# Attention times v in plain fp32 on two column tiles of TensorE, one a head

## The chip, the core and the metric

The kernel runs on one core of a Trainium2 chip. The metric is the time of one execution in microseconds (us), the median over executions. The core has five engines that run side by side: TensorE (PE; its weight loads are shown apart as PEld), VectorE (DVE), ScalarE (ACT), GpSimd (POOL) and SyncE (SP), which issues all of this kernel's DMAs. TensorE's clock is granted at one of two levels, 1.2 or 2.4 GHz; the profile gives the granted clock as a share of 2.4 GHz.

## The reference

```python
q_rot, k_rot = (rotate(q), rotate(k))                     # 4 batches, 8 heads, 576 positions, 64 wide
scores = scale * np.matmul(q_rot, k_rot.transpose(0, 1, 3, 2))
scores = scores - np.max(scores, axis=-1, keepdims=True)
attn = np.exp(scores)
attn = attn / (np.sum(attn, axis=-1, keepdims=True) + 1e-09)
x = np.matmul(attn, v)                                    # heads side by side: 2304 x 512
h = x @ w_in                                              # 512 x 2048
P = a[0] + a[1] * h + a[2] * h**2 + a[3] * h**3
Q = 1.0 + np.abs(b[0]) * np.abs(h) + np.abs(b[1]) * h**2
out = (P / (Q + 1e-06)) @ w_out                           # 2048 x 512
```

Attention with rotated q and k comes first, then a feed-forward part with a rational function in the place of an activation. All is fp32.

## The kernel before

**Attention** goes over 16 pairs of heads; 16 pairs take 16 turns. For a pair p these steps are made, each a named step of the program:

- `ld`, `ro0` to `ro2`: load q and k, rotate them (GpSimd). `hi` (ScalarE) writes the rounded half of q and k into the buffer `q2`, `lo` (GpSimd) what is left over, as fp32r. The DMAs `kh`, `kl` move k's halves from `q2` to `ks`, and `qh`, `ql` then copy q's halves over the place in `q2` where k's halves stood, so `qh` waits until `kh` has landed and `ql` until `kl` has. `q2` has two buffers: `hi` of pair p waits for the last scores of pair p-2. There are two buffers for loaded x, given back by `lo`.
- `s0` to `s8` (line 453): the scores, nine blocks of 128 rows for the two heads together; 42 matmuls a pair. `m0` to `m8` take the row maxima (VectorE, line 461), `x0` to `x8` the exponentials and their sums (ScalarE, line 468). The score banks in PSUM are two.
- `tA`, `tB`, `tJ`, `tL` (line 511): 45 transposes of 128 columns in eleven groups, most of four, one PSUM bank a group, three banks. `hA`, `hB`, ... (ScalarE, line 528) copy a bank's rounded half to `eh`, `lA`, `lB`, ... (VectorE, line 530) write what is left over to `el`; both must be done before the bank is free.
- `vh` and `vl` (ScalarE and GpSimd, lines 431 and 434) split v in the same way into `vv`, the halves side by side: 128 columns.
- `av0` to `av3` (line 541): for each head and half of the positions ten matmuls of 288 columns, five with `eh` and five with `el`, against `vv`. So the sum with v's high half comes out in 64 rows of the bank and that with its low half in the other 64. `ac` (ScalarE) copies the lower rows out, `aa` (VectorE) adds the two. There is one such bank.
- `n0` to `n4`: the reciprocal sums, turned by a transpose (`n1`, line 480), sent to DRAM and back spread over 64 rows (`n3`, `n4`). `f0` (GpSimd) multiplies by them, `f1` stores the result for the feed-forward part.

**Feed-forward** runs in 73 units. A unit has twelve matmuls of 512 columns into a bank `h` (line 816), a chain of some twelve steps on ScalarE, VectorE and GpSimd, and twelve matmuls into four banks `acc` (lines 864 to 866). Its weights come in a packed form and take some six steps each on ScalarE, VectorE and GpSimd before they can be used. The first units `h0` to `h3` stand between the last steps of attention, because the banks `acc` need the PSUM that attention gives back after its last `av`.

**Order.** Nothing on the chip chooses: each engine takes its instructions in the order written. That order comes from a table of due times (`SLOTS`, in ninths of a turn, with tables of their own for pairs 0, 1, 14 and 15, and `DUE` for the feed-forward part) and from a planner that goes through the steps with a time for each; the due times give the order in which ready steps are taken. The times in the planner are the author's and are not used here as evidence.

Of the kernel before, what the change touches and what calls it, by code (L numbers as in the profile page):

```python
# [1140 lines left out]
```

## Time and profile before

| | |
|---|---|
| time, median of 3 executions | 721.39 us (719.87 to 724.22) |
| span of the profiled execution, first to last instruction | 718.0 us |
| TensorE busy | 680.2 us (95%) |
| VectorE busy | 578.5 us (81%) |
| ScalarE busy | 584.9 us (81%) |
| GpSimd busy | 447.8 us (62%) |
| mean granted clock of TensorE | 0.985 |

The profile's span ends at the last instruction and has no time of its own for what lies around it; the median of the shown executions is 3.4 us above it. Busy time is an average over stages. Matmuls overlap in the pipeline and their ends are modelled, so the pace of TensorE is read from the distance between starts, not from the duration of one.

### The profile page before, as it was taken

The page shows a single profiled execution, that of the slowest core. Times are in us where ns is not written, and L with a number is a line of the kernel's source. Part 1 is how long each engine was busy: PE and PEld are TensorE (multiplying, and loading weights), DVE is VectorE, ACT ScalarE, POOL GpSimd, SP SyncE. Part 2 cuts the span into 40 slices and gives each one's busy share as a digit, 9 for nine tenths or more (in the row PEclk, how much of TensorE's full clock was granted, in tenths as well). Part 3 has the DMA queues.
Part 4 walks back from the last instruction along what each step waited for, and adds up shares of the span by engine and source line. Part 5 has one row for each costly group of instructions (what it writes and reads, how often), then busy time and mean ns, then how long its engine had stood idle before and what let it go on. Part 6 is the DMA issues. An engine that isn't in the chain of part 4 may idle for free.

```text
span 718.0 us, 11373 instructions
## 1 busy us (share of the span) xinstructions
PE 680.2 (95%) x3864; PEld 586.6 (82%) x3864; DVE 578.5 (81%) x941; ACT 584.9 (81%) x1110; POOL 447.8 (62%) x295
## 2 busy tenths in 40 slices
PE   6698999999999998969999999999999999999997
PEld 2587998999999997858787888888888888888896
DVE  5798888989889989997998998986766667666685
ACT  1598899999999999987998997988777777776774
POOL 0567778788788847486676766767544554444422
PEclk9699999999999999989999999999999999999999
DMA  9758787887887665352434234323100010000100
GB/s 251 213 123 212 176 210 189 191 194 193 216 188 212 162 186 178 106 174 104 150 115 147 89 132 146 119 97 124 51 0 1 7 45 16 0 1 0 48 13 30
DMA packets 34649, 86.34 MB, mean 120 GB/s; under 512 B 5008, under 2 KB 8224, under 8 KB 32672
## 3 DMA queue, kind: packets, MB, share of 16 engines
q1 hardware_dynamic: 34592, 85.62, 42.8%
q8 instruction: 31, 0.51, 0.3%
q14 instruction: 26, 0.21, 0.1%
HBM read 55.25 MB, written 12.66 MB: 95 GB/s over the span
## 4 chain that ended last, share of the span: by engine, by line
PE 72%; DMA 14%; ACT 5%; DVE 5%; issue 1%; POOL 1%; SPq 1%; DVEq 0%; POOLq 0%; ACTq 0%
PE h L816 26%; PE acc L866 9%; PE acc L865 9%; PE acc L864 9%; PE s L453 7%; DMA ks<-q 7%; PE av L541 6%; DMA q<-q 4%; PE t_B L511 3%; ACT e L468 2%; PE t_A L511 2%; DMA const<-in_b_dram 1%; ACT eh L528 1%; PE t_J L511 1%; DMA tab<-in_tab_dram 1%
## 5 line engine op out<-in xcount | busy, mean ns | idle before, releaser
L453 PE MATMUL s<-ks,q 128*128 128x288 f32 (+2 forms) x672 | 121.4, 311 | 22.4 <-DVE ks L402 8.5
L849 POOL TENSOR_TENSOR gl<-u,gh 128x512 fp32r<-128x512 f32 (+1 forms) x73 | 93.8, 1286 | 75.9 <-ACT gh L848 59.8
L840 POOL TENSOR_TENSOR v<-v,t 128x512 f32<-128x512 f32 x68 | 88.6, 1303 | 83.9 <-ACT v L838 82.8
L461 DVE TENSOR_REDUCE nm<-s 128x1 f32<-128x576 f32 x144 | 107.9, 752 | 24.5 <-PE s L453 22.3
L453 PEld LDWEIGHTS s<-ks,q 128*128 128x128 f32 x672 | 97.0, 194 | 30.1 <-ACT e L468 11.2
L468 ACT ACTIVATE e<-s,nm 128x576 f32<-128x576 f32 x144 | 107.0, 743 | 12.8 <-DVE nm L461 8.3
L541 PE MATMUL av<-eh,vv 128*128 128x288 f32 x320 | 91.3, 308 | 6.5 <-DVE xo L558 6.5
L866 PE MATMUL acc<-woh,gl 128*128 128x512 f32 x234 | 92.4, 395 | 0.2 <-POOL gl L849 0.2
L865 PE MATMUL acc<-wol,gh 128*128 128x512 f32 x234 | 92.4, 395 | 0.0
L864 PE MATMUL acc<-woh,gh 128*128 128x512 f32 x234 | 92.3, 394 | 0.0
L541 PE MATMUL av<-el,vv 128*128 128x288 f32 x320 | 87.7, 297 | 0.0
L837 ACT ACTIVATE t<-h 128x512 f32<-128x512 f32 (+1 forms) x73 | 43.1, 591 | 47.4 <-PE h L816 47.1
L845 DVE SCALAR_TENSOR_TENSOR v<-v,p 128x512 f32<-128x512 f32 (+1 forms) x73 | 49.5, 678 | 39.2 <-ACT p L844 37.8
L841 DVE TENSOR_TENSOR u<-u,h 128x512 f32<-128x512 f32 (+1 forms) x73 | 49.5, 678 | 37.4 <-ACT u L839 37.1
L816 PE MATMUL h<-xh,wih 128*128 128x512 f32 (+1 forms) x204 | 75.1, 368 | 0.1
L816 PE MATMUL h<-xh,wil 128*128 128x512 f32 (+1 forms) x204 | 74.9, 367 | 0.0
L816 PE MATMUL h<-xl,wih 128*128 128x512 f32 (+1 forms) x204 | 74.7, 366 | 0.0
L379 POOL TENSOR_TENSOR x<-x,tab 128x1152 f32<-128x1152 f32 x28 | 74.4, 2663 | 0.0
L541 PEld LDWEIGHTS av<-eh,vv 128*128 128x128 f32 x320 | 60.7, 190 | 7.7 <-ACT xh L789 3.9
L848 ACT ACTIVATE gh<-u 128x512 fp32r<-128x512 f32 (+1 forms) x73 | 45.5, 623 | 20.1 <-PE acc L865 15.2
L541 PEld LDWEIGHTS av<-el,vv 128*128 128x128 f32 x320 | 61.0, 191 | 0.0
L838 ACT ACTIVATE v<-t,const 128x512 f32<-128x512 f32 (+1 forms) x73 | 59.1, 809 | 2.0
(114 smaller groups left out, 1721.6 us busy)
## 6 DMA issues: line engine op xcount, KB each, us to landing
x<-in_qk_dram SPq DMA_DIRECT2D x15, 1152.0 KB
ks<-q SPq DMA_DIRECT2D x30, 288.0 KB, 5.7
q<-q SPq DMA_DIRECT2D x30, 288.0 KB, 4.6
rawi<-in_w_in_dram SPq DMA_DIRECT2D x16, 512.0 KB
rawo<-in_w_out_dram SPq DMA_DIRECT2D x16, 512.0 KB, 3.5
vf<-in_v_dram SPq DMA_DIRECT2D x16, 320.0 KB, 7.5
rb<-rd SPq DMA_DIRECT2D x32, 144.0 KB, 3.8
xd<-xo SPq DMA_DIRECT2D x16, 288.0 KB, 2.1
```

The source lines that it names most:

```text
L379: eng.tensor_tensor(x[:, :, i], x[:, :, i], t, ALU.mult)
L453: nc.tensor.matmul(ps[:, half, x:x + k.shape[-1]], q, k, start=(i == 0), stop=(i == len(ops) - 1))
L461: self.nc.vector.tensor_reduce(nm, st["s", c][:, :, :HALF], AX.XY, ALU.max, negate=True)
L468: self.nc.scalar.activation(e.rearrange("p (a b) -> p a b", a=2), st["s", c][:, :, :HALF], AF.Exp, bias=st["nm", c], scale=1.0, accum_out= ...
L541: nc.tensor.matmul(po[:, :HALF], v, e, start=(i == 0), stop=(i == len(ops) - 1))
L816: self.nc.tensor.matmul(ph[:, i * n:(i + 1) * n], w[:, k * P:(k + 1) * P], x[:, :n], start=(j == 0), stop=(j == len(terms) - 1))
L838: "v": lambda: act(new("v"), d["t"], AF.Identity, bias=self.b[0], scale=self.b[1]),
L840: "w": lambda: (nc.gpsimd.tensor_tensor if u < POOL_W else tt)(d["v"], d["v"], d["t"], ALU.mult),
L849: "gl": lambda: (nc.gpsimd.tensor_tensor(new("gl", F32R), d["u"], fp(d["gh"]), ALU.subtract), self.g.update({u: (d["gh"], d["gl"])})),
L864: nc.tensor.matmul(acc, gh[:, c], hi, start=(first and i == 0), stop=False)
L865: nc.tensor.matmul(acc, gh[:, c], lo, start=False, stop=False)
L866: nc.tensor.matmul(acc, gl[:, c], hi, start=False, stop=(last and i == len(fs) - 1))
```

## The change

`av` has two steps a pair in place of four, one for each half of the positions. In each, ten plain fp32 matmuls write 64 rows each, head 0 to rows 0 to 63 of the bank (column tile 0 of TensorE), head 1 to rows 64 to 127 (column tile 1), in turn. Their operands are the exponentials and v as they are. So `vh`, `vl`, all eleven `l` steps, the four `aa` and two of the four `ac` are gone. A transposed bank is copied out once: five of the eleven groups by ScalarE (`ON_ACT`), six by VectorE. `ac0` copies a finished bank on ScalarE, `ac1` on VectorE. The reordering of head 1's positions, which `aa` did on the way, is now done by the DMAs: `n4` has three DMAs and not two, `f1` three and not one. v's buffers are two (from one), given back after `av`. All due times are set anew.

```diff
-    "s1": -68.81, "s3": -68.34, "ld": -67.83, "s2": -67.47, "s0": -65.53, "s4": -65.09, "s5": -64.79,
...
+    "s1": -66.68, "s2": -66.17, "s3": -64.59, "s0": -64.09, "s4": -63.78, "s5": -63.24, "tA3": -62.77,
...
+ON_ACT = ("A0", "A2", "B0", "B2", "J1")
...
-        "vh": ("A", 0.70, ["ldv"]), "vl": ("G", 1.50, ["vh"]),
...
-        "f0": ("G", 1.4, ["aa0", "aa1", "aa2", "aa3", "n4"]), "f1": ("S", 0, ["f0"], (1, 1.0)),
+        "n3": ("S", 0, ["n2"], (1, 0.1)), "n4": ("S", 0, ["n3"], (3, 1.5)),
+        "f0": ("G", 1.4, ["ac0", "ac1", "n4"]), "f1": ("S", 0, ["f0"], (3, 1.0)),
...
-        st["h" + g] = "A", 0.1 if g == "J1" else 0.48, ["t" + g]
-        st["l" + g] = "D", 0.135 if g == "J1" else 0.6, ["h" + g]
...
+        a = g in ON_ACT
+        st["h" + g] = "DA"[a], (0.135, 0.24)[a] if g == "J1" else (0.6, 0.6)[a], ["t" + g]
+    for i in range(2):
+        st[f"av{i}"] = "P", 2.5, ["ldv"] + ["h" + g for g in of if i or not g.startswith(("L", "J1"))]
+        st[f"ac{i}"] = "AD"[i], (0.43, 0.37)[i], [f"av{i}"]
...
-        "t": (3, [("t" + g, ["l" + g]) for g in of] + [("n1", ["n2"])]),
-        "v": (1, [(f"av{i}", [f"aa{i}"]) for i in range(4)]),
...
+        "t": (3, [("t" + g, ["h" + g]) for g in of] + [("n1", ["n2"])]),
+        "v": (1, [(f"av{i}", [f"ac{i}"]) for i in range(2)]),
...
-            for h in range(2):
-                nc.sync.dma_start(rb[h * D:(h + 1) * D],
-                                  flat[h * S:(h + 1) * S].partition_broadcast(D))
+            nc.sync.dma_start(rb[:D], flat[:S].partition_broadcast(D))
+            nc.sync.dma_start(rb[D:, :S - D], flat[S + D:].partition_broadcast(D))
+            nc.sync.dma_start(rb[D:, S - D:], flat[S:S + D].partition_broadcast(D))
...
+        if f"{kind}{j}" in ON_ACT:
+            nc.scalar.activation(to, pv, AF.Copy)
+        else:
+            nc.vector.tensor_copy(to, pv)
...
+        po = st["v", half] = self.ps_v.tile([P, 512], F32, tag="v", name=f"av{p}_{half}")
+        c = slice(half * HALF, (half + 1) * HALF)
+        for j in range(5):
+            for h in range(2):
+                v = st["vf"][:, 4 * h + j if j < 4 else 8 + h]
+                e = st["et"][:, j, h, c] if j < 4 else st["et4"][:, c]
+                nc.tensor.matmul(po[h * D:(h + 1) * D, :HALF], v, e, start=(j == 0), stop=(j == 4))
...
+        to, po = st["xo"][:, half * HALF:(half + 1) * HALF], st["v", half][:, :HALF]
+        if half == 0:
+            nc.scalar.activation(to, po, AF.Copy)
+        else:
+            nc.vector.tensor_copy(to, po)
...
-            nc.sync.dma_start(self.x_dram[b][:, hp, :], x)
+            to = self.x_dram[b][:, hp, :]
+            nc.sync.dma_start(to[:D], x[:D])
+            nc.sync.dma_start(to[D:, D:], x[D:, :S - D])
+            nc.sync.dma_start(to[D:, :D], x[D:, S - D:])
```

**The order on ScalarE**, before, at the end of the scores of pair 8 (`s8_8`, `s8_7` are score banks, `e` the exponentials, `q2` is shown as `q20`, x10 is the loaded pair 10):

```order
L468 ACTIVATE e_96,sum0_107<-s8_8_2225,nm8_8_2237 128x576
L528 ACTIVATE eh8_2182<-t8_A_0_2248 128x512
L468 ACTIVATE e_96,sum0_107<-s8_7_2241,nm8_7_2263 128x576
L528 ACTIVATE eh8_2182<-t8_A_1_2258 128x512
L549 ACTIVATE xt7_2_2289<-av7_2_2265 64x288
L413 ACTIVATE q20_99<-x10_1860 128x2x576
L468 ACTIVATE e_96,sum1_108<-s9_1_2281,nm9_1_2296 128x576
```

The same place now:

```order
L443 ACTIVATE e_96,sum0_107<-s8_6_1836,nm8_6_1851 128x576
L501 ACTIVATE et8_1828<-t8_A_0_1854 128x512
L397 ACTIVATE q20_99<-x10_1537 128x2x576
L443 ACTIVATE e_96,sum0_107<-s8_8_1860,nm8_8_1872 128x576
L443 ACTIVATE e_96,sum0_107<-s8_7_1874,nm8_7_1894 128x576
L523 ACTIVATE xo7_1905<-av7_0_1880 128x288
L443 ACTIVATE e_96,sum1_108<-s9_1_1900,nm9_1_1912 128x576
```

`hi` of pair 10 (the row with `q20`) stood behind the last two exponentials of pair 8 and two copies; now it stands ahead of those exponentials.

**The order of DMAs on SyncE**, before, for one turn (`ks11<-q21` are `kh` and `kl` of pair 11, `q21<-q21` its `qh` and `ql`, x13 the load of pair 13, `xd` is `f1`, `rb` is `n4`, `rd` is `n3`):

```order
L421 DMA ks11_2544<-q21_100 64x2x576
L352 DMA x13_2598<-in_qk_dram 128x2304
L421 DMA ks11_2544<-q21_100 64x2x576
L425 DMA q21_100<-q21_100 64x2x576
L372 DMA vf11_2661<-in_v_dram 128x640
L486 DMA rd9_2683<-rr9_2663 9x128
L425 DMA q21_100<-q21_100 64x2x576
L568 DMA xd2_62<-xo8_2445 128x576
L491 DMA rb9_2745<-rd9_2683 64x576 x2
```

The same turn now:

```order
L405 DMA ks11_2091<-q21_100 64x2x576 x2
L336 DMA x13_2137<-in_qk_dram 128x2304
L409 DMA q21_100<-q21_100 64x2x576
L465 DMA rb8_2161<-rd8_2018 64x576
L466 DMA rb8_2161<-rd8_2018 64x512
L467 DMA rb8_2161<-rd8_2018 64x64
L535 DMA xd1_61<-xo7_1905 64x576
L536 DMA xd1_61<-xo7_1905 64x512
L537 DMA xd1_61<-xo7_1905 64x64
L409 DMA q21_100<-q21_100 64x2x576
L356 DMA vf10_2208<-in_v_dram 128x640
L461 DMA rd9_2218<-rr9_2206 9x128
```

`kl` now stands ahead of the large load of x and not behind it; `ql` stands behind that load and behind six small DMAs.

**The order on TensorE** now, from the last scores of pair 9 to the middle of the scores of pair 10 (`av8_0` and `av8_1` are the two halves of pair 8; before, four steps of ten matmuls of 128x288 each stood at four places of a turn):

```order
L428 MATMUL s9_7_2074<-ks9_1691,q21_100 128x288 x4
L515 MATMUL av8_0_2080<-et8_1828,vf8_1808 64x288 x8
L515 MATMUL av8_0_2080<-et4_8_1829,vf8_1808 64x288 x2
L428 MATMUL s10_1_2100<-ks10_1891,q20_99 128x288 x4
L428 MATMUL s10_2_2107<-ks10_1891,q20_99 128x288 x4
L485 MATMUL t9_J_0_2114<-ident_98,e_96 128x128 x4
L485 MATMUL t9_A_2_2122<-ident_98,e_96 128x128 x4
L485 MATMUL t9_B_3_2132<-ident_98,e_96 128x128 x4
L428 MATMUL s10_3_2139<-ks10_1891,q20_99 128x288 x4
L515 MATMUL av8_1_2148<-et8_1828,vf8_1808 64x288 x8
L515 MATMUL av8_1_2148<-et4_8_1829,vf8_1808 64x288 x2
```

The first half of `av` now fills the place between the last scores of a pair and the first of the next, and each half is entered from and left for matmuls that use all 128 columns.

## Rows read from the trace of the kernel before

**Rows 1.** The page's first line.
```profile
span 718.0 us, 11373 instructions
```

**Rows 2.** Windows: stretch, length, busy us of each engine, granted clock, DMA share, GB/s.
```profile
12.00:30.00 18.00, 7.30 (x28) 5.64 (x27) 15.58 (x22) 7.17 (x14) 4.38 (x3) 0.65 1.02 275
...
200.00:250.00 50.00, 49.01 (x385) 47.37 (x383) 45.09 (x84) 47.29 (x111) 42.38 (x20) 1.00 0.76 188
...
300.00:350.00 50.00, 43.46 (x199) 36.14 (x198) 43.85 (x70) 42.22 (x72) 37.62 (x29) 0.93 0.43 144
...
550.00:600.00 50.00, 50.00 (x218) 40.64 (x217) 32.98 (x48) 38.03 (x61) 26.14 (x23) 1.00 0.07 24
```

**Rows 3.** The chain that ended last: start us, us, what.
```profile
97.53 1.45 PE av L541 x10
...
162.81 1.19 PE s L453 x10
...
170.54 0.87 PE t_A L511 x8
171.42 1.32 PE av L541 x10
172.92 1.17 PE s L453 x7
...
246.57 1.44 PE av L541 x10
```

**Rows 4.** Waits of TensorE from 60 to 262 us: total, times, longest.
```profile
PE s L453 <- DMA q<-q: 5.5, 6, 1.5
```

**Rows 5.** Timeline at one turn's `hi`, `kl` and `ql`, and the scores ahead.
```profile
152.90 0.77 PE L453 MATMUL s<-ks,q 128*128 128x288 f32 x4
...
156.52 1.15 ACT L413 ACTIVATE q<-x 128x1152 fp32r<-128x1152 f32 x1
...
160.83 0.63 SPq L421 DMA_DIRECT2D ks<-q  x1
...
168.75 0.60 SPq L425 DMA_DIRECT2D q<-q  x1
```

**Rows 6.** Timeline of TensorE, first scores of the program.
```profile
21.86 2.29 PE L453 MATMUL s<-ks,q 128*128 128x288 f32 x8 [8.48 <-DVE ks L402]
```

**Rows 7.** Waits of TensorE from 20 to 60 us.
```profile
PE s L453 <- ACT e L468: 3.7, 5, 1.4
```

**Rows 8.** Waits of TensorE from 262 to 325 us.
```profile
PE av L541 <- DVE xo L558: 6.5, 2, 3.7
```

**Rows 9.** Timeline of TensorE, from the last scores to the end of attention.
```profile
289.95 0.80 PE L453 MATMUL s<-ks,q 128*128 128x288 f32 x4 [0.20 <-ACT e L468]
...
311.66 0.58 PE L541 MATMUL av<-eh,vv 128*128 128x288 f32 x1 [3.67 <-DVE xo L558]
...
321.64 1.06 PE L816 MATMUL h<-xh,kept 128*128 128x512 f32 x2
...
325.84 0.39 PE L864 MATMUL acc<-kept,gh 128*128 128x512 f32 x1
```

**Rows 10.** Timeline of TensorE, two neighbours of the feed-forward part.
```profile
348.56 0.39 PE L864 MATMUL acc<-kept,gh 128*128 128x512 f32 x1
348.79 0.39 PE L865 MATMUL acc<-kept,gh 128*128 128x512 f32 x1
```

**Rows 11.** Timeline of TensorE, first two matmuls of an `av` after transposes.
```profile
171.17 0.38 PE L541 MATMUL av<-eh,vv 128*128 128x288 f32 x1
171.39 0.29 PE L541 MATMUL av<-el,vv 128*128 128x288 f32 x1
```

**Rows 12.** Groups of instructions by form: count, then busy us, mean ns, idle before.
```profile
L530 DVE TENSOR_TENSOR el<-t_B,eh 128x512 fp32r<-128x512 f32 x64 | 43.6, 683 | 3.1 <-ACT eh L528 3.0
...
L528 ACT ACTIVATE eh<-t_A 128x512 fp32r<-128x512 f32 x64 | 38.3, 602 | 4.2 <-PE t_A L511 4.1
...
L434 POOL TENSOR_TENSOR vv<-vf,vv 128x640 fp32r<-128x640 f32 x16 | 25.5, 1596 | 35.0 <-ACT vv L431 34.8
```

More of the change, by code (lines that the diff above doesn't have):

```diff
@@ L119 @@
 DUE = {
[5 rows of a table removed]
[5 rows of a table added]
 }
 DUE_0 = {
-    "t": -7.80, "v": 396.31, "w": -9.41, "u1": 399.03, "u2": -351.99, "ln": -346.35, "u3": 427.36,
-    "ex": -358.45, "e": -342.95, "r": -56.25, "g": 416.20, "gh": 6.97, "gl": 446.65, "down": 388.26,
-    "flush": -36.80,
+    "t": 87.18, "v": -412.07, "w": -395.95, "u1": 403.30, "u2": -404.80, "ln": 350.49, "u3": 350.69, "ex": -390.03,
+    "e": -404.05, "r": 347.92, "g": -394.16, "gh": -372.41, "gl": 380.37, "down": 400.34, "flush": -394.20,
 }
 DUE_1 = {
-    "roq": -274.70, "rok": 447.98, "hiq": 438.00, "hik": 440.39, "loq": 463.53, "lok": -305.02,
+    "roq": -200.11, "rok": -125.06, "hiq": -121.35, "hik": -162.42, "loq": -202.88, "lok": -135.20,
 }
@@ L259, in attention_steps @@
         "qh": ("S", 0, ["kh", "lo"], (1, 1.55)), "ql": ("S", 0, ["kl"], (1, 1.55)),
[1 row of a table removed]
         "n0": ("D", 0.33, [f"x{c}" for c in range(NBLK)]), "n1": ("P", 0.11, ["n0"]), "n2": ("A", 0.16, ["n1"]),
-        "n3": ("S", 0, ["n2"], (1, 0.1)), "n4": ("S", 0, ["n3"], (2, 1.5)),
-        "f0": ("G", 1.4, ["aa0", "aa1", "aa2", "aa3", "n4"]), "f1": ("S", 0, ["f0"], (1, 1.0)),
+        "n3": ("S", 0, ["n2"], (1, 0.1)), "n4": ("S", 0, ["n3"], (3, 1.5)),
+        "f0": ("G", 1.4, ["ac0", "ac1", "n4"]), "f1": ("S", 0, ["f0"], (3, 1.0)),
     }
@@ L272, in attention_steps @@
         st["t" + g] = "P", 0.219 if g == "J1" else 0.437, [f"x{c}" for c in cs]
-        st["h" + g] = "A", 0.1 if g == "J1" else 0.48, ["t" + g]
-        st["l" + g] = "D", 0.135 if g == "J1" else 0.6, ["h" + g]
-    for i, kinds in enumerate((("A", "J0"), ("A", "L", "J"), ("B", "L", "J0"), ("B", "J"))):
-        st[f"av{i}"] = "P", 1.36, ["vl"] + ["l" + g for g in of if g.startswith(kinds)]
-        st[f"ac{i}"] = "A", 0.43, [f"av{i}"]
-        st[f"aa{i}"] = "D", 0.5 if i == 3 else 0.42, [f"ac{i}"]
-    avs, scores = [f"av{i}" for i in range(4)], [f"s{c}" for c in range(NBLK)]
+        a = g in ON_ACT
[3 more added lines that the diff above has]
+        st[f"ac{i}"] = "AD"[i], (0.43, 0.37)[i], [f"av{i}"]
+    avs, scores = [f"av{i}" for i in range(2)], [f"s{c}" for c in range(NBLK)]
     holds = {
         "s": (2, [(f"s{c}", [f"x{c}"]) for c in range(NBLK)]),
-        "t": (3, [("t" + g, ["l" + g]) for g in of] + [("n1", ["n2"])]),
-        "v": (1, [(f"av{i}", [f"aa{i}"]) for i in range(4)]),
-        "x": (2, [("ld", ["lo"])]), "vf": (1, [("ldv", ["vl"])]),
-        "vv": (2, [("vh", avs)]), "xt": (2, [(f"ac{i}", [f"aa{i}"]) for i in range(4)]),
+        "t": (3, [("t" + g, ["h" + g]) for g in of] + [("n1", ["n2"])]),
+        "v": (1, [(f"av{i}", [f"ac{i}"]) for i in range(2)]),
+        "x": (2, [("ld", ["lo"])]), "vf": (2, [("ldv", avs)]),
         "rb": (1, [("n4", ["f0"])]),
@@ L289, in attention_steps @@
     back["hi"] = [(2, a) for a in scores]
-    back.update({f"aa{i}": [(2, "f1")] for i in range(4)})
+    back.update({f"ac{i}": [(2, "f1")] for i in range(2)})
     back["x4"] = [(1, "tL0"), (1, "tJ1")]
@@ L347, in __init__ @@
         nc.gpsimd.memset(self.both[D:], 1.0 / K_SCALE)
-        self.x0 = fp(self.p2.tile([P, 4, 2, S], F32R, tag="el", name="x0"))
+        self.x0 = self.p2.tile([P, 4, 2, S], F32, tag="et", name="x0")
     def load(self, p):
@@ L370, in load_v @@
         nc, st = self.nc, self.st[p]
-        vf = st["vf"] = self.p2.tile([P, NBLK + 1, D], F32, tag="vf", bufs=1, name=f"vf{p}")
+        vf = st["vf"] = self.p2.tile([P, NBLK + 1, D], F32, tag="vf", name=f"vf{p}")
         nc.sync.dma_start(vf, self.v[p])
@@ L425, in copy_q @@
         self.nc.sync.dma_start(fp(q2[D:, t, :, :S]), fp(q2[:D, t, :, :S]))
-    def split_v(self, p, lo):
-        st, vf = self.st[p], self.st[p]["vf"]
-        if not lo:
-            st["vv"] = self.p2.tile([P, NBLK + 1, P], F32R, tag="vv", name=f"vv{p}")
-            self.nc.scalar.activation(st["vv"][:, :, :D], vf, AF.Copy)
-        else:
-            vv = st["vv"]
-            self.nc.gpsimd.tensor_tensor(vv[:, :, D:], vf, fp(vv[:, :, :D]), ALU.subtract)
     def scores(self, p, c):
@@ L496, in transposes @@
         kind, j = g
-        if "eh" not in st:
-            for n in ("eh", "el"):
-                st[n] = self.p2.tile([P, 4, 2, S], F32R, tag=n, name=f"{n}{p}")
-                st[n + "4"] = self.p2.tile([P, S], F32R, tag=n + "4", name=f"{n}4_{p}")
+        if "et" not in st:
+            st["et"] = self.p2.tile([P, 4, 2, S], F32, tag="et", name=f"et{p}")
+            st["et4"] = self.p2.tile([P, S], F32, tag="et4", name=f"et4_{p}")
         pt = st["t", g] = self.ps_t.tile([P, 512], F32, tag="t", name=f"t{p}_{kind}_{j}")
@@ L511, in transposes, with copy_e @@
             nc.tensor.transpose(pt[:e.shape[-1], x:x + P], e, self.ident)
-    def split_e(self, p, g, lo):
+    def copy_e(self, p, g):
         nc, st = self.nc, self.st[p]
@@ L517, in split_e @@
         if kind == "J":
-            c = slice(0, 4 * P) if j == 0 else slice(4 * P, S)
-            hi, el = st["eh4"][:, c], st["el4"][:, c]
+            to = st["et4"][:, :4 * P] if j == 0 else st["et4"][:, 4 * P:]
             if j == 1:
@@ L523, in split_e @@
             pv = pv.rearrange("p (j h c) -> p j h c", j=4, h=2)
-            hi, el = (st[n][:, :, :, 4 * P:] for n in ("eh", "el"))
+            to = st["et"][:, :, :, 4 * P:]
         else:
-            hi, el = (st[n][:, j, "AB".index(kind), :4 * P] for n in ("eh", "el"))
-        if not lo:
-            nc.scalar.activation(hi, pv, AF.Copy)
-        else:
-            nc.vector.tensor_tensor(el, pv, fp(hi), ALU.subtract)
-    def av(self, p, q):
+            to = st["et"][:, j, "AB".index(kind), :4 * P]
@@ L533, in av @@
+        if f"{kind}{j}" in ON_ACT:
+            nc.scalar.activation(to, pv, AF.Copy)
+        else:
+            nc.vector.tensor_copy(to, pv)
+    def av(self, p, half):
         nc, st = self.nc, self.st[p]
-        h, half = divmod(q, 2)
-        po = st["v", q] = self.ps_v.tile([P, 512], F32, tag="v", name=f"av{p}_{q}")
-        c0 = half * HALF
-        ops = [(st["vv"][:, 4 * h + j], st[n][:, j, h, c0:c0 + HALF])
-               for j in range(4) for n in ("eh", "el")]
-        ops += [(st["vv"][:, 8 + h], st[n][:, c0:c0 + HALF]) for n in ("eh4", "el4")]
@@ L540, in av @@
-        for i, (v, e) in enumerate(ops):
-            nc.tensor.matmul(po[:, :HALF], v, e, start=(i == 0), stop=(i == len(ops) - 1))
-    def av_out(self, p, q, i):
-        nc, st = self.nc, self.st[p]
-        h, half = divmod(q, 2)
-        po = st["v", q]
-        if i == 0:
-            t = st["xt", q] = self.p2.tile([D, HALF], F32, tag="xt", name=f"xt{p}_{q}")
-            nc.scalar.activation(t, po[D:P, :HALF], AF.Copy)
-        else:
-            if "xo" not in st:
-                st["xo"] = self.pa.tile([P, S], F32, tag="xo", name=f"xo{p}")
-            c0 = half * HALF
-            cols = [(0, HALF, c0)] if h == 0 else [(0, HALF, D)]
-            if q == 3:
-                cols = [(0, 4 * P - c0, c0 + D), (4 * P - c0, HALF, 0)]
-            for a, b, t in cols:
-                nc.vector.tensor_tensor(st["xo"][h * D:(h + 1) * D, t:t + b - a],
-                                        po[:D, a:b], st["xt", q][:, a:b], ALU.add)
+        po = st["v", half] = self.ps_v.tile([P, 512], F32, tag="v", name=f"av{p}_{half}")
@@ new lines, in av, with av_out @@
+        c = slice(half * HALF, (half + 1) * HALF)
[4 more added lines that the diff above has]
+                nc.tensor.matmul(po[h * D:(h + 1) * D, :HALF], v, e, start=(j == 0), stop=(j == 4))
+    def av_out(self, p, half):
+        nc, st = self.nc, self.st[p]
+        if "xo" not in st:
+            st["xo"] = self.pa.tile([P, S], F32, tag="xo", name=f"xo{p}")
+        to, po = st["xo"][:, half * HALF:(half + 1) * HALF], st["v", half][:, :HALF]
+        if half == 0:
+            nc.scalar.activation(to, po, AF.Copy)
+        else:
+            nc.vector.tensor_copy(to, po)
@@ L572, in ops @@
              "kh": lambda p: self.move_k(p, 0), "kl": lambda p: self.move_k(p, 1),
-             "qh": lambda p: self.copy_q(p, 0), "ql": lambda p: self.copy_q(p, 1),
-             "vh": lambda p: self.split_v(p, 0), "vl": lambda p: self.split_v(p, 1)}
+             "qh": lambda p: self.copy_q(p, 0), "ql": lambda p: self.copy_q(p, 1)}
         for i in range(3):
@@ L582, in ops @@
             o[f"n{i}"] = lambda p, i=i: self.norm(p, i)
-        for i in range(4):
+        for i in range(2):
             o[f"av{i}"] = lambda p, i=i: self.av(p, i)
-            o[f"ac{i}"] = lambda p, i=i: self.av_out(p, i, 0)
-            o[f"aa{i}"] = lambda p, i=i: self.av_out(p, i, 1)
-        for i in range(2):
+            o[f"ac{i}"] = lambda p, i=i: self.av_out(p, i)
             o[f"f{i}"] = lambda p, i=i: self.finish(p, i)
@@ L591, in ops @@
             o["t" + n] = lambda p, g=g: self.transposes(p, g)
-            o["h" + n] = lambda p, g=g: self.split_e(p, g, 0)
-            o["l" + n] = lambda p, g=g: self.split_e(p, g, 1)
+            o["h" + n] = lambda p, g=g: self.copy_e(p, g)
         return o
@@ L1076, in switch_back @@
         ffn.open_rest(left2)
-    pairs, ends = range(NP), [f"aa{i}" for i in range(4)]
+    pairs, ends = range(NP), ["ac0", "ac1"]
     prog.add("top", "", 0, 0, switch_top, [(n, p) for p in pairs[-2:] for n in ("lo", "kh", "kl", "qh", "ql")])
```

123 rows, old and new, of tables (DUE, SLOTS, SLOTS_0, SLOTS_1) are left out of this document.

## The prediction

> **What bounds the kernel now.** The page gives a span of 718.0 us [rows 1]. I read the windows first, because the kernel has stages with different limits [rows 2]. From 550 us on, in the feed-forward part, TensorE is busy for all 50 us of 50 and the rest has room: that stage changes only if its start moves. In a window of the middle of attention, TensorE has 49.0 us, but VectorE 45.1, ScalarE 47.3 and GpSimd 42.4 as well: four engines near their limit. The start (clock 0.65, TensorE busy for 7.3 of 18 us) and the change to the feed-forward part (43.5 of 50 us, clock 0.93) are loose. So the question is what TensorE does in attention and at its end.
>
> *A turn.* The chain of work shows the pace without the modelled ends [rows 3]: ten matmuls of an `av` in 1.32 us (0.132 each), eight transposes in 0.87 (0.109 each), the ten of `s4` in 1.19. A pair is then worth, on TensorE, 32 x 0.132 + 1.19 = 5.41 us of scores, 45 x 0.109 + 0.1 = 5.0 of transposes and 40 x 0.132 = 5.28 of `av`: 15.69 us. Two `av` steps nine turns apart start at 97.53 and 246.57 [rows 3], so a turn takes 16.56 us. It loses 0.87 us to gaps. Part of that is a wait that the page names, scores for the copy of q [rows 4]; the rest are gaps too short for that list, before transposes and scores whose bank is not yet free.
>
> *The loop behind that wait* [rows 5]. Pair p-2's last scores start at 152.90 and end, at 0.132 each, at 153.4. `hi` of pair p could start there and starts at 156.52, behind exponentials and copies on ScalarE. `kl` is issued at 160.83, just behind the load of x, and `ql`, which waits until `kl` has landed, at 168.75. The scores of pair p go on at 172.92 [rows 3]. That is 19.5 us, and they are waited for: the loop is just as long as TensorE's turn allows.
>
> *Start and end.* The first scores start at 21.86 [rows 6]. In the filling of the pipeline scores wait for exponentials for 3.7 us [rows 7]. At the end two `av` steps of the last pair wait 6.5 us together for VectorE to add out the step before [rows 8], behind feed-forward work. The last scores start at 289.95 and end at 290.5; attention ends at 321.64 [rows 9]. In these 31.1 us stand 7 groups of transposes (3.1), six `av` steps (7.9) and four units `h` (48 matmuls x 0.229 = 11.0, the pace being 50 us / 218 from rows 2): 22.0 of work, 9 of gaps. The unit behind it takes 4.2 us (321.64 to 325.84), where 12 x 0.229 = 2.75 is the pace: it runs at the lower clock after the waits.
>
> **The change, part by part.** From 21.86 to 321.64 TensorE takes 299.8 us, of which 16 x 15.69 + 11.0 = 262.0 is work and 37.8 gaps: 13 turns x 0.87 = 11.3 in the middle, 9 at the end, 17.5 in the filling and the rest.
>
> *The matmuls.* Removed are 640 matmuls of 0.132 us: 84.5 us. Added are 320 in plain fp32 with 64 columns of weights; no row shows one. One of them does what one with `eh` and one with `el` did for 128 columns: four products of a high or low half. *Lower bound*: it runs at the pace of the old ones and two tiles at once, 10 x 0.132 / 2 = 0.66 us a step. *Upper bound*: the four products one after the other and the tiles too. From 0.23 us between neighbours of 512 columns [rows 10] and 0.132 for 288, a column costs 0.00043 and a matmul about 0.007 beside; four products are 4 x 0.125 + 0.007 = 0.507, and ten in a row 5.07 us. I take four products and the two tiles at once, since old and new then use the array's columns equally: 2.53 us a step, or 2.64 if the fixed part is paid four times. Mean 2.58, so 5.16 a pair where there was 5.28: almost nothing is won here. The gain has to come from gaps.
>
> *Changes of tile.* Each step is entered and left: 4 a pair, 64 in all. No row shows a change of tile. The first `av` matmul after transposes takes 0.22 us to the next one where 0.132 is the pace [rows 11]; I take that 0.09 for each, 5.8 us. Bounds: nothing, and the 0.38 that the first one is shown for, less 0.132: 0.25 each, 16 us. The Trainium skill (TensorEngine Tiling (Array Packing), Tiling Modes) says that changing the tiling mode drains TensorE, which speaks against the change. It gives no price; with the row's 0.25 for a drain the sum would be 716.
>
> *The copies.* VectorE loses 11 `l` steps a pair (0.68 each) and four adds, and gets six copies and one of a finished bank. ScalarE goes from eleven copies (0.60) to five, from four `ac` to one, and loses `vh`; GpSimd loses `vl`, 1.6 us [rows 12]. In a turn VectorE and ScalarE so fall from about 15 us to 11, GpSimd to 12. All of this lay beside TensorE and is worth nothing by itself, but a transposed bank is free after one copy and not two in a row, and `av` after one copy. I leave 0.2 us of gap a turn: 2.6 in place of 11.3 (bounds: 0 and 11.3).
>
> *The loop* has to let that happen. `hi` now waits on ScalarE for the last scores alone, so some 2.9 us are won. `kl` no longer stands behind the load, but `ql` does, and behind the six small DMAs of `n4` and `f1`. From `kl` on, 288 + 1152 + 4 x 288 KB must pass, 2.65 MB; at 188 GB/s for a share of 0.76 [rows 2], 247 GB/s, that is 10.7 us. Before, load and `kl`, 1.47 MB, took 7.9 us from issue to landing, 6.0 at that rate, so 1.9 are latency. With the 4.3 us from `hi` to the issue of `kl` [rows 5] the loop takes 17 us, an estimate. It may take a turn, 16.1 by this sum, plus the first half of `av`, which now stands between the two pairs' scores: 18.7. It is hidden, with 1.7 us to spare. `n4` waits for `f0`, and SyncE's queue with it, `ql` too; GpSimd does `f0` directly behind `lo`, so it is done before `n4` comes up. The three DMAs more a pair cost SyncE some 0.6 us each, hidden in its free time.
>
> *End.* Work: the same transposes and units, and four steps `av` of 2.58. The bank is now freed by one copy, with a unit `h` between the two steps of the last pair: the 6.5 us go. I leave 2.5 of gap for 9, and 1.4 us for the unit at the lower clock are won. *Filling*: VectorE's first row maximum comes about 1 us later, since a rest of the rotation stands ahead of it; ScalarE's `vh` and copies among the exponentials go. I take 3 us off.
>
> *Sum.* Work 16 x (5.41 + 5.0 + 5.16) + 11.0 = 260.1; changes of tile 5.8; gaps 2.6 + 2.5 + 14.5 = 19.6; together 285.5, which is 14.3 less than 299.8. With the 1.4 behind it, the profiled execution falls from 718.0 to 702.3 us. The median of the runs is 3.4 above the span, so **706 us**.
>
> **The rivals.** *The tiles do not run at once.* Then a step takes 5.07 us, 32 steps cost 80 us more, and the time is 786: slower. It decides where a step takes more than 2.58 + 15.7 / 32 = 3.07. For it: no row of this trace has two matmuls at once. Against it: nothing but that their columns and their PSUM rows differ. *They overlap only in part.* From 3.07 to 3.6 us a step the time goes from 721 to 739. The Trainium skill (TensorE: Matmul & The Clock Gate, Part 3) reports 2.38 times for three column tiles; two at that share give 1.59 times, 5.07 / 1.59 = 3.19 us a step and 725 us. No run here shows it. *The gaps stay*, because the loop, which was just long enough to bind, takes over 18.7 us with six more DMAs ahead of `ql`, or because each change of tile costs 0.25 us: 13 x 0.67 = 8.7, or 10, on top: 715 or 716. For it: the copy of q is the one wait that the page names in the middle; against it: `hi` starts 2.9 us earlier.
>
> **How the numbers follow.** Forecast 0.66, its own range 695 (no cost for a change of tile, no gaps) to 719 (0.25 for each); gaps stay 0.08; partly at once 0.12; one after the other 0.14. 8 in 10 lie between 695 and 735, which leaves out the serial case and the ends. A measurement of this kernel can tell 0.5% from no change, 717.8 to 725.0. Faster: 0.66 and half of the gaps case, 0.70; same: 0.04 of the gaps, 0.04 of the partial case, 0.08; slower: the rest, 0.22.
>
> **What would show it.** In the changed kernel's chain, a step `av` of 2.5 to 2.65 us from its first matmul to the next instruction's; over 3.07 the forecast falls. The starts of `av` and of the row behind it give the change of tile. The turn should be 15.8 to 16.3 us, the wait for the copy of q should be gone from the middle, VectorE and ScalarE should stand near 34 us of 50 there. At the end no wait of `av` for VectorE, and attention ending near 307 us. If the span of the stage behind attention is not the old 396 us, the start of the feed-forward part was not what I moved.

## The result, and the profile after

The changed kernel takes 712.94 us (median of 3 runs, 712.72 to 713.36) against 721.39 before: 0.9878 times, with a 95% interval of 0.9835 to 0.9921. That is faster, by 8.5 us or 1.2%, where 15.4 us were forecast. The profiled execution's span is 710.9 us, 7.1 less than before [rows 1].

In the rows of the changed kernel, L386 and L401 are low parts of k and q, L363 and L365 the rotation, L428 the scores, L436 the row maxima, L443 the exponentials, L485 the transposes and L515 `av`. The windows, for three stretches of [rows 2]:

```profile
12.00:30.00 18.00, 2.06 (x10) 1.62 (x8) 17.38 (x17) 4.08 (x6) 8.02 (x3) 0.60 0.65 178
200.00:250.00 50.00, 50.00 (x396) 40.63 (x396) 34.62 (x59) 35.00 (x82) 36.84 (x16) 1.00 0.73 186
300.00:350.00 50.00, 46.30 (x218) 34.65 (x217) 43.21 (x68) 43.20 (x72) 38.74 (x30) 1.00 0.48 155
```

In the middle TensorE is busy for 50.00 us of 50 (49.01 before), with VectorE at 34.6 and ScalarE at 35.0. From 300 to 350 us it gained 2.8 us of work and the full clock. From 12 to 30 us it lost: 2.06 us of work where there were 7.30. This is all that its list of waits from 60 to 262 us has left (total, times, longest; 5.5 us for the copy of q in [rows 4]):

```profile
PE rt L455 <- DVE rs L452: 0.2, 1, 0.2
```

A turn in the chain of work (start, us, what):

```profile
153.51 0.53 PE s L428 x4
154.04 2.58 PE av L515 x20
156.62 1.25 PE s L428 x8
...
159.91 2.58 PE av L515 x20
162.49 0.72 PE s L428 x4
...
169.94 2.58 PE av L515 x20
```

An `av` step takes 2.58 us (1.32 to 1.45 before, with twice as many steps [rows 3]). Its ten matmuls are 20 records, since each plain fp32 matmul stands in the trace as two. A turn goes from 154.04 to 169.94, 15.90 us (16.56 before).

The start, from the timeline (start, us, engine; in brackets what ended the idle time before):

```profile
21.90 5.81 POOL L363 TENSOR_TENSOR x<-x,tab 128x1152 f32<-128x1152 f32 x2 [20.04 <-DMA x<-in_qk_dram]
27.79 3.04 POOL L365 TENSOR_TENSOR x<-x 128x1152 f32<-128x1152 f32 x1
...
22.19 6.14 DVE L386 SCALAR_TENSOR_TENSOR ks<-x,ks 64x576 fp32r<-64x576 f32 x2
28.36 3.69 DVE L401 TENSOR_TENSOR q<-x,q 128x1152 fp32r<-128x1152 f32 x1
31.97 1.41 DVE L436 TENSOR_REDUCE nm<-s 128x1 f32<-128x576 f32 x2
...
28.38 2.29 PE L428 MATMUL s<-ks,q 128*128 128x288 f32 x8 [15.94 <-DVE ks L386]
```

The first scores come at 28.38 (21.86 before [rows 6]). The low parts of k of pair 0 take 6.14 us for two on VectorE, and the low part of pair 1 takes 3.69, while GpSimd rotates pair 2; VectorE's steps end 0.6 and 1.2 us after GpSimd's (28.33 after 27.71, 32.05 after 30.83). In the kernel before, the same engines stand so in the timeline:

```profile
25.62 1.53 POOL L434 TENSOR_TENSOR vv<-vf,vv 128x640 fp32r<-128x640 f32 x1 [23.76 <-ACT vv L431]
27.12 5.24 POOL L379 TENSOR_TENSOR x<-x,tab 128x1152 f32<-128x1152 f32 x2
...
21.05 0.76 DVE L402 SCALAR_TENSOR_TENSOR ks<-x,ks 64x576 fp32r<-64x576 f32 x1
...
23.30 0.75 DVE L461 TENSOR_REDUCE nm<-s 128x1 f32<-128x576 f32 x1
```

There a low part of k takes 0.76 us, the first row maximum comes at 23.30, and `vl` of pair 0, which is gone now, stands ahead of GpSimd's rotation and waits for ScalarE until 25.62.

The end of attention, from the timeline:

```profile
312.52 0.50 PE L829 MATMUL acc<-kept,gh 128*128 128x512 f32 x1
...
320.74 0.50 PE L831 MATMUL acc<-kept,gl 128*128 128x512 f32 x1 [1.84 <-POOL gl L814]
...
324.40 0.73 PE L781 MATMUL h<-xh,kept 128*128 128x512 f32 x2 [1.10 <-DVE u L807]
```

Attention ends at 312.52 (321.64 before [rows 9]), and no `av` waits for VectorE any more; behind it, two new waits of the feed-forward units.

### The profile page after: what moved, and what is told of

Its sections match the earlier page's. It is cut to its first block, busy times and chain, and to the rows that moved or that the text cites. A ratio compares the mean times of both kernels' runs of the same rounds, so it can differ in the third digit from the quotient of the medians.

```text
span 710.9 us, 11008 instructions
## 1 busy us (share of the span) xinstructions
PE 675.3 (95%) x3864; PEld 544.0 (77%) x3864; DVE 528.4 (74%) x797; ACT 512.8 (72%) x950; POOL 423.4 (60%) x279
## 4 chain that ended last, share of the span: by engine, by line
PE 87%; DVE 5%; DMA 3%; ACT 3%; issue 1%; SPq 0%; POOL 0%; DVEq 0%; ACTq 0%; POOLq 0%
PE h L781 27%; PE s L428 13%; PE av L515 11%; PE acc L831 9%; PE acc L830 9%; PE acc L829 9%; PE t_B L485 4%; PE t_A L485 4%; DMA x<-in_qk_dram 1%; PE t_J L485 1%; ACT e L443 1%; PE t_L L485 1%; DMA tab<-in_tab_dram 1%; DVE ks L386 1%; DVE nm L436 1%
## 5 line engine op out<-in xcount | busy, mean ns | idle before, releaser
L443 ACT ACTIVATE e<-s,nm 128x576 f32<-128x576 f32 x144 | 106.2, 738 | 79.8 <-DVE nm L436 75.3
L436 DVE TENSOR_REDUCE nm<-s 128x1 f32<-128x576 f32 x144 | 107.9, 750 | 73.0 <-PE s L428 42.3
L428 PE MATMUL s<-ks,q 128*128 128x288 f32 (+2 forms) x672 | 121.1, 317 | 21.2 <-DVE ks L386 15.9
L428 PEld LDWEIGHTS s<-ks,q 128*128 128x128 f32 x672 | 96.4, 196 | 38.5 <-DVE ks L386 16.4
L363 POOL TENSOR_TENSOR x<-x,tab 128x1152 f32<-128x1152 f32 x28 | 74.2, 2671 | 20.0 <-DMA x<-in_qk_dram 20.0
L515 PE MATMUL av<-et,vf 128*64 128x288 f32 x640 | 84.7, 411 | 0.0
L401 POOL TENSOR_TENSOR q<-x,q 128x1152 fp32r<-128x1152 f32 x14 | 37.1, 2652 | 63.3 <-ACT q L397 58.9
L515 PEld LDWEIGHTS av<-et,vf 128*64 128x64 f32 x640 | 43.1, 137 | 30.9 <-issue 2.8
L804 ACT ACTIVATE u<-h,const 128x512 f32<-128x512 f32 (+1 forms) x73 | 55.3, 758 | 2.0 <-POOL gl L814 1.9
```

What stands on the lines that cost most here:

```text
L363: eng.tensor_tensor(x[:, :, i], x[:, :, i], t, ALU.mult)
L428: nc.tensor.matmul(ps[:, half, x:x + k.shape[-1]], q, k, start=(i == 0), stop=(i == len(ops) - 1))
L436: self.nc.vector.tensor_reduce(nm, st["s", c][:, :, :HALF], AX.XY, ALU.max, negate=True)
L443: self.nc.scalar.activation(e.rearrange("p (a b) -> p a b", a=2), st["s", c][:, :, :HALF], AF.Exp, bias=st["nm", c], scale=1.0, accum_out= ...
L515: nc.tensor.matmul(po[h * D:(h + 1) * D, :HALF], v, e, start=(j == 0), stop=(j == 4))
```

## Experiments

Ratios are to the kernel before, run beside each experiment, with 95% intervals.

**The wait that was only planned.** Theory A is that VectorE's two-input steps and GpSimd's exclude each other. The edit gives the rotation two predecessors in the planner:

```
+                if (n, p) == ("ro0", 2):
+                    after += [("lo", 0, "k", 1), ("lo", 1)]
```

> The changed kernel, with one wait more: GpSimd's first rotation of pair 2 starts only when VectorE has done the low parts of k of pair 0 and the low part of pair 1; the order on every engine stays as it was. Theory A (VectorE's two-input steps and GpSimd's exclude each other, so GpSimd's early rotation stretches VectorE's last three steps from 2.9 to 9.8 us): the two low parts of k take 0.75 us each and that of pair 1 takes 1.35, first scores near 23.1 us where they were at 28.4, first row maximum near 25.1 where it was 32.0, and the time 5 to 7 us lower, 706 to 708 us. Rival B (the start is late because of the order of VectorE's steps and the landing of the loads of x0): VectorE's steps keep their length, nothing moves, 713 us. Rival C (what is won there is lost again, because pair 2's q and k come some 4 us later): first scores at 23.1, but a wait of the scores of pair 2, and 710 to 714 us.

Measured: 712.24 us, 0.9871 (0.9846 to 0.9896), and the start as before the edit. GpSimd starts at 21.91 (21.90 without the edit). The planner's list only sets an order, the order was the same already, and no wait came of it. The run says nothing on the theories and stands as a repeat of the changed kernel.

**VectorE's order.** The low part of pair 1 goes behind the first row maxima:

```
+                if (n, p) == ("lo", 1):
+                    after += [("m1", 0), ("m2", 0)]
```

> The changed kernel with the low part of pair 1 on VectorE moved behind the first row maxima of pair 0; GpSimd is left as it is. Theory A: the low parts of k still take 6.1 us beside GpSimd's rotation and the first scores stay at 28.4; the row maxima, which read PSUM, run at 0.7 us beside GpSimd, so the first one comes near 29 where it was 32.0; at most 3 us of gain, 710 to 712 us. Rival B (the place of the low part of pair 1 in VectorE's order is the loss): the whole 6 us come back, near 707 us.

> Both edits: GpSimd's rotation of pair 2 waits for VectorE's low parts, and the low part of pair 1 stands behind the first two row maxima. Theory A: first scores near 23.1, first row maximum near 23.9, the low part of pair 1 again 1.35 us; 0 to 1.5 us below the run with the wait alone, 705 to 708 us. If GpSimd's rotation is now so late that pair 2 is waited for (rival C), it is slower than the run with the wait alone.

Measured: 712.43 us, 0.9874 (0.984 to 0.9909), and 711.43, 0.9863 (0.9837 to 0.9889). In the second the planned wait was again without effect, so both test the order alone. The low parts of k still take 6.14 and 6.17 us. The low part of pair 1 comes when GpSimd is done and takes 1.36 us, the first row maximum starts at 29.5 and 29.9, but the scores then wait 2.9 and 0.8 us for the copy of q of pair 1. Rival B falls: the order is worth 1 us or so.

**GpSimd really held.** Ahead of the rotation GpSimd reads one number per partition that VectorE writes last (the edit but for the allocation of `junk`):

```
         if i < 2:
+            if (p, i) == (2, 0):
+                eng.tensor_copy(self.junk, fp(self.q2[1][:, 1, 1, S - 1:S]))
             t = self.tab[:, i:i + 1, :].to_broadcast([P, 2, S])
```

The planner's two predecessors stay in. The order of instructions on every engine is that of the changed kernel, with this one copy put in.

> The changed kernel, with GpSimd now really held: ahead of its first rotation of pair 2 it copies one number per partition out of the low part of pair 1, which VectorE writes last, so it cannot start before VectorE is done. (The first try set the order alone, which was the same as before, and GpSimd started at 21.9 as before.) Theory A: the two low parts of k take 1.5 us together where they took 6.1, that of pair 1 1.35 where it took 3.7; first scores near 23.1 us (28.4), first row maximum near 25.1 (32.0); the time 5 to 7 us lower, 706 to 708 us. Rival B (VectorE's steps are long for another reason, such as DMA traffic): they keep their length, and nothing moves but GpSimd, which starts at 32: 713 us or more. Rival C: first scores at 23.1, but the scores of pair 2 wait for the late rotation, 710 to 714 us.

Measured: **705.65 us**, 0.9771 (0.9747 to 0.9794), the lowest time of this study. Its timeline:

```profile
22.04 1.43 DVE L386 SCALAR_TENSOR_TENSOR ks<-x,ks 64x576 fp32r<-64x576 f32 x2
23.50 1.36 DVE L401 TENSOR_TENSOR q<-x,q 128x1152 fp32r<-128x1152 f32 x1
23.52 2.29 PE L428 MATMUL s<-ks,q 128*128 128x288 f32 x8 [10.01 <-DVE ks L386]
...
24.88 0.76 DVE L436 TENSOR_REDUCE nm<-s 128x1 f32<-128x576 f32 x1
...
24.92 0.18 POOL L361 COPY junk<-q 128x1 f32<-128x1 f32 x1 [23.05 <-DVE q L401]
25.06 5.21 POOL L363 TENSOR_TENSOR x<-x,tab 128x1152 f32<-128x1152 f32 x2
...
305.76 0.50 PE L829 MATMUL acc<-kept,gh 128*128 128x512 f32 x1
```

The same steps take 1.43 and 1.36 us, GpSimd begins 3.2 us later, and attention ends 6.8 us earlier, at 305.76. Row maxima beside the rotation stay at 0.76 us; they have one input, in PSUM, and which of the two spares them is not tested. Theory A holds, rival B falls, and pair 2 is not waited for (C).

**Both, with the real hold.** Expected and measured:

> The same hold on GpSimd, and the low part of pair 1 behind the first two row maxima. Theory A: first scores near 23.1 us, first row maximum near 24, the low part of pair 1 1.35 us; GpSimd starts near 27, as in the kernel before; 705 to 708 us. Rival C: pair 2 is waited for, and it is slower than the run with the hold alone.

706.62 us, 0.9782 (0.976 to 0.9804): no better than the hold alone. The scores wait 1.0 us for the copy of q, but of pair 1 and not of pair 2.

**The kernel before, without its protection.** One number in a table of due times:

```
-    "vl": -65.41,
+    "vl": 30.5,
```

> The kernel before, with the low part of v of pair 0 moved behind GpSimd's rotation of pair 2, by one due time. In the kernel before it stood ahead of it and waited for ScalarE until 25.6 us, which kept GpSimd out of VectorE's way. Theory A: GpSimd starts near 21 to 22 us, VectorE's two-input steps from then on (half a rotation and a low part of k and of q, four of 0.75 us) take up to 3 us each, and the row maxima behind them come 5 us or more later than in the kernel before. Rival B (these steps are long in the changed kernel for a reason of its own): they stay at 0.75 us. The later program is ordered a little differently too, so the end time, near 721 to 728 us, tells less than the start.

Measured: 736.59 us (one run), beside 721.38. The timeline of its start:

```profile
21.11 3.16 DVE L402 SCALAR_TENSOR_TENSOR ks<-x,ks 64x576 fp32r<-64x576 f32 x1
24.31 3.08 DVE L386 TENSOR_TENSOR x<-x,tab 128x576 f32<-128x576 f32 x1
27.31 1.41 DVE L461 TENSOR_REDUCE nm<-s 128x1 f32<-128x576 f32 x2
...
21.05 5.72 POOL L379 TENSOR_TENSOR x<-x,tab 128x1152 f32<-128x1152 f32 x2 [19.19 <-DMA x<-in_qk_dram]
```

The same two steps took 0.76 us each in the kernel before: the stretch is there without any part of the change. The first row maximum comes 4.0 us later (27.31 for 23.30), where 5 or more were expected. The time is above the expected range too; only the start is read from this run, since its later order differs (the stage behind the last `av` takes 407.8 us where it took 396.6).

**Two tiles at once?** The loops around the `av` matmuls are exchanged:

```
-        for j in range(5):
-            for h in range(2):
+        for h in range(2):
+            for j in range(5):
```

> The changed kernel with the two loops around the av matmuls exchanged: the five matmuls of one head come first, then the five of the other, so that neighbours in TensorE's queue lie on the same column tile, with the same matmuls, tiles and PSUM rows. Theory A (a pair of neighbours runs at once because it lies on two tiles): a step takes 9 to 10 times 0.5 us, 4.6 to 5.1 us where it took 2.58, a turn near 20.5 us, and the time some 32 x 2.3 = 74 us higher, 775 to 795 us. Rival (a plain fp32 matmul with 64 columns costs 0.26 us by itself): 2.58 us a step as before and 713 us.

Measured: 757.38 us (one run). A step takes less than expected in its chain:

```profile
150.47 4.08 PE av L515 x20
```

The weight loads in the timeline tell why; first those of the changed kernel, then those of this one:

```profile
154.27 0.14 PEld L515 LDWEIGHTS av<-et,vf 128*64 128x64 f32 x2
154.51 0.14 PEld L515 LDWEIGHTS av<-et,vf 128*64 128x64 f32 x2
```

```profile
151.18 0.14 PEld L515 LDWEIGHTS av<-et,vf 128*64 128x64 f32 x1
151.43 0.14 PEld L515 LDWEIGHTS av<-et,vf 128*64 128x64 f32 x1
...
151.91 0.14 PEld L515 LDWEIGHTS av<-et,vf 128*64 128x64 f32 x2
...
152.40 0.14 PEld L515 LDWEIGHTS av<-et,vf 128*64 128x64 f32 x1
152.45 0.14 PEld L515 LDWEIGHTS av<-et,vf 128*64 128x64 f32 x1
```

In the changed kernel two start together every 0.24 us; here one does, except from 151.91 to 152.45, where loads of the second head run beside the first head's last three. Of the matmul records in the trace, the first head's last four and the second head's first four start side by side (from 151.91 to 152.69). So 16 starts of 0.243 us are left of 20, 3.9 us; with 0.16 for the change of tile, which the next run gives, that is 4.05. The rival, 2.58 us a step in any order, falls.

**No tiles.** v is padded with zeros to 128 columns, and both heads add up in one bank:

```
-                nc.tensor.matmul(po[h * D:(h + 1) * D, :HALF], v, e, start=(j == 0), stop=(j == 4))
+                nc.tensor.matmul(po[:, :HALF], v, e, start=(j + h == 0), stop=(j + h == 5))
```

> The changed kernel without column tiles: v is padded with zeros to 128 columns, the one head in the left half and the other in the right, so that ten plain fp32 matmuls per step, as many as before, add up in one bank with both heads. The load of v is twice as large. Theory A (four products in plain fp32, 0.483 us a matmul as two records of 0.242 in one tile show): 4.85 us a step, no change of tile, 74 us more, 780 to 790 us. Rival (plain fp32 takes two products, and it is the weight loads that alternating tiles hide): 2.6 us a step and 713 us.

Measured: 776.0 us (one run). The chain:

```profile
156.06 4.85 PE av L515 x20
160.91 1.05 PE s L428 x8
...
164.03 4.85 PE av L515 x20
168.88 0.53 PE s L428 x4
```

A record takes 4.85 / 20 = 0.243 us with 128 columns of weights, as on one tile with 64, and the two tiles hide every second one. The rival, 2.6 us a step, falls. The scores behind `av` take 1.05 and 0.53 us here, 1.25 and 0.72 in the changed kernel: leaving the column tiles costs 0.19 to 0.20 us. Entering them is put at the rest of the step, 2.58 - 4.85 / 2 = 0.16.

**Which relief closed the gaps of the middle?** First the high part of pair p is moved back (`"hi": 66.05` to `68.55` in the main table), then the banks are read twice:

> The changed kernel with the high part of the next pair but one put back on ScalarE behind exponentials and a copy, some 3 us later, as it stood in the kernel before; nothing else. By the trace of the changed kernel the loop from the high part to the landing of the last copy of q takes 13.2 us of 18.5 that it may take: no new wait, 712 to 714 us. By the prediction's own estimate (17 of 18.7) scores would wait 1.3 us a turn for the copy of q, a turn of 17.2 us, and 725 to 730 us.

Measured: 734.38 us, 1.0165 (1.0139 to 1.0191), slower than the kernel before and above both expectations. TensorE's waits from 60 to 262 us, and two rows of ScalarE:

```profile
PE s L428 <- ACT e L443: 9.5, 9, 1.4
PE s L428 <- DMA q<-q: 7.2, 7, 3.4
```

```profile
154.01 0.41 ACT L523 ACTIVATE xo<-av 128x288 f32<-128x288 f32 x1 [2.62 <-DMA xd<-xo]
154.32 1.16 ACT L397 ACTIVATE q<-x 128x1152 fp32r<-128x1152 f32 x1
```

The scores wait for q again. From the first scores of pair 3 (83.72) to those of pair 13 (257.64) a turn takes 17.4 us, near the 17.2 of the second expectation. The high part came 5.6 us after the last scores (they end at 148.70, and in the changed kernel it follows at once), not 3: it stood behind a copy that waited for a store, and exponentials stood behind it; the order of the DMAs moved with it. The 13.2 us of the first expectation were too short as well: in the changed kernel one high part starts at 138.09, its `ql` is issued at 150.55, and the packets of that copy run until about 153.5, so the loop takes 15.4 us of 18.5.

Then the banks; the step that is added (the lines that order it are left out):

```
+    def read_again(self, p, g):
+        to = self.p2.tile([P, 512], F32, tag="again", name=f"again{p}_{g[0]}{g[1]}")
+        c = slice(D, P) if g == ("J", 1) else slice(0, 512)
+        self.nc.vector.tensor_copy(to[:, c], self.st[p]["t", g][:, c])
```

> The changed kernel, in which VectorE reads each of the five transposed banks that ScalarE copies once more, into a buffer that nobody uses: a bank is free only after two copies in a row, as before, and VectorE has 9 us of 50 more to do; the place of the high part and the DMAs stay as they are. Theory D (the gaps closed because a bank is free after one copy): transposes wait for banks again, a turn of 16.2 to 16.6 us where it took 15.90, 717 to 722 us. Theory E (the gaps closed because the loop of q became short): no new gap, a turn of 15.9, 712 to 714 us.

Measured: 738.22 us, 1.0249 (1.0212 to 1.0285). The chain, and TensorE's longest wait from 60 to 262 us:

```profile
116.26 2.58 PE av L520 x20
...
167.00 2.58 PE av L520 x20
```

```profile
PE t_A L487 <- DVE again_B L510: 2.4, 12, 0.6
```

Three turns take 50.74 us, 16.91 each, with no wait for q: theory D's kind of gap, and larger than it said (1.0 us a turn for five banks of eleven). Some 13 of the 25 us lie in the 13 turns. Of the rest, 9 lie behind the last `av` (407.6 us for 398.8), where the planner's order changed and one unit `h` more stands. Second copies and VectorE's load rose together here (39.5 us of 50 from 200 to 250 us; 34.6 in the changed kernel, 45.1 before); which of them costs the 1.0 us stays open.

So either of the two, loop or banks, can bind by itself. How the old loss of 0.87 us a turn divided between them is not shown, since both runs gave back more than the change had won: in the kernel before, the high part stood 3.1 us behind the scores and not 5.6. Of that loss [rows 4] name 5.5 us in 202, some 0.45 a turn, as waits for q.

**The half clock at the start.** In the run with the hold, the granted clock is 0.50 from 20 to 30 us. `WARM`, the count of idle matmuls, goes from 40 to 70, then to 92 with all ahead of the scores:

> The changed kernel with GpSimd held (as in the run that gave 705.65 us), and with 70 in place of 40 idle matmuls ahead of the first scores, which then keep TensorE busy until some 22 us where they ended at 13.5 and the granted clock fell to a half until 33. If the half clock is what is left of the loss at the start, the 30 score matmuls of the first nine steps take 0.13 and not 0.27 us each, some 4 us less, of which the waits for exponentials take back up to 2: 702 to 704 us. If VectorE and ScalarE set the pace there, 705 to 706 us.

> As the run before, with 92 idle matmuls, all ahead of the first scores. With 70 they ended at 18.5 us (0.24 us each, not 0.29), TensorE then sat idle for 5.3 us, and the clock was at a half again when the scores came at 23.8. With 22 more at 0.213 us they should end near 23.2. If the half clock is what is left of the loss at the start: granted clock 1.0 from 20 to 30 us, the first eight score matmuls in 1.06 us where they took 2.29, and 702 to 704 us. If the pace of row maxima and exponentials sets the end there, 705 to 706 us with the same clock.

Measured: 706.3 us, 0.9806 (0.9774 to 0.9838), and 706.02, 0.9778 (0.976 to 0.9796). In the first the idle matmuls ended too early to tell. The windows and the timeline of the second:

```profile
20.00:25.00 5.00, 4.58 (x25) 2.47 (x22) 4.94 (x7) 1.65 (x3) 0.00 (x0) 1.00 0.71 180
25.00:30.00 5.00, 2.41 (x13) 1.80 (x12) 3.08 (x5) 3.11 (x8) 4.71 (x3) 0.89 0.62 149
30.00:40.00 10.00, 9.46 (x53) 8.72 (x53) 5.79 (x9) 5.36 (x14) 3.29 (x2) 0.71 0.40 132
```

```profile
23.89 1.34 PE L428 MATMUL s<-ks,q 128*128 128x288 f32 x8 [0.42 <-DVE ks L386]
26.82 1.51 PE L428 MATMUL s<-ks,q 128*128 128x288 f32 x8 [1.59 <-ACT e L443]
```

The first scores do run at the full clock (1.00 from 20 to 25 us), then wait for row maxima and exponentials, and behind that wait the clock is lower again (0.89, then 0.71). Nothing is won: in this stretch the exponentials set the pace, as the second reading said.

## Why the prediction was right in sign and 7 us off

**The `av` step: right in time, by two errors that cancel.** 2.58 us was forecast for the matmuls alone, and 2.58 measured with the entry into the tiles in it. A matmul takes 0.485 us (2 x 0.243) where 0.507 was estimated from four products; the size fits, but the trace shows two records and not what is done in them. Ten of them on two tiles at once are 2.43 us, and entering adds 0.16. The rival "not at once" was over-priced: 776 us without tiles, not 786. "In part" falls: inside a step the overlap is complete. The Trainium skill (TensorE: Matmul & The Clock Gate, Part 3) reports 2.38 times for three column tiles; no run here has three, two gave 4.85 / 2.58 = 1.88 with the change of tile in it.

**The changes of tile: right in sum, half the price.** I put 0.09 us on each of four a pair, 0.36. Measured are 0.16 on entering and 0.19 to 0.20 on leaving, 0.7 a pair. That the sum came out is luck: the matmuls were 0.3 a pair cheaper than forecast, and 0.38 of the changes lie outside the 2.58. The Trainium skill (TensorEngine Tiling (Array Packing), Tiling Modes) says that a change of tiling mode drains TensorE; the rows agree in that each change has a price, about 0.35 us for the two of a step, and do not show what happens in it. The forecast's range has a slip here: 0.25 on each change gives 716, as the rivals say, and not its upper end of 719.

**The turn and the loop: right.** Forecast 16.13 us with 0.2 of gap, measured 15.90 with none. VectorE and ScalarE stand at 35 of 50 (34 was said), and the wait for the copy of q is gone. The loop takes 15.4 us where 17 was estimated.

**The end: half right.** The two waits of `av` for VectorE, 6.5 us, are gone. But the span behind 312.52 is 398.4 us where it was 396.4 behind 321.64, with the same work of TensorE in it (four units `h` stand ahead in both), and I had taken 1.4 off. That is 3.4 us on the wrong side. Waits for gl (1.84) and u (1.10) stand there now; why these come late is not tested.

**The filling: the step that failed.** The prediction says: "Filling: VectorE's first row maximum comes about 1 us later ... I take 3 us off." It came 8.7 us later (31.97 for 23.30) and the first scores 6.5. I counted `vl` of GpSimd as work beside TensorE, worth nothing. But it was also a lock on the rotation: it waited for ScalarE until 25.6 us and kept GpSimd's rotation away from VectorE's last two-input steps. With it gone, the rotation starts as soon as its load lands, and I had priced those steps by rows in which GpSimd was still. The held run shows the size: 1.43 + 1.36 us for 6.14 + 3.69, and 6.4 us of span (704.5 for 710.9). Even there the first row maximum comes 1.6 us later than before (24.88), near the forecast's 1, and the first scores 1.7 (23.52), which I had put at nothing; the new order on VectorE is left as a cause, and no run undoes it. The Trainium skill (SBUF — State Buffer, Who interferes with whom) states this rule, that a VectorE instruction with two SBUF inputs and a GpSimd instruction that reads SBUF exclude each other for the whole instruction; the rows agree, with steps of 0.75 us stretched to 3.1 in the changed kernel and in the kernel before without `vl` in its place, and not stretched with GpSimd held.

**The account** in spans: forecast 702.3, measured 710.9. First scores later, 6.5; attention from there on 284.1 us where 285.5 was forecast, -1.4; behind it, 3.4: together 8.5. The median stood 2.0 above the span where I had 3.4, so the time is 6.9 off; that 1.4 is luck, since 3.4 set the median of three executions beside the span of another one (the profiled execution here has 712.72 us and a span of 710.9, 1.8 apart). With GpSimd held it is 705.65, beside a forecast of 706, but part of that agreement is luck too: the 3.4 behind attention are still lost there (398.7 us behind 305.76).

## What to carry to other kernels

When a step is removed, ask what stood behind it in its queue, and what that will now run beside: a step that only waited may have been a lock that nobody wrote down. A predecessor in a planner's list made no wait on the chip here (GpSimd at 21.91 us, as without it); a copy of one number per partition did (25.06). Where a loop and a buffer both stand near the pace, either can bind by itself: tightening one alone took more than the whole gain here (734 and 738 us).
